# Loads from GpSimd with one packet per transfer and engine

## The chip, the cores and the metric

The kernel runs on one core of a Trainium2 chip. The metric is the device time of one execution, in microseconds (us). The core has five engines that matter here, each with its own list of instructions: TensorE (PE; its weight loads are listed apart as PEld), VectorE (DVE), ScalarE (ACT), GpSimd (POOL) and SyncE (SP). Transfers between the chip's memory (DRAM) and the core's on-chip memory (SBUF) are carried out by 16 DMA engines. They are asked for by GpSimd, whose transfers may change the number type on the way, or by SyncE[...].

## The reference

Two layers follow each other. Batch is 8, heads 8, sequence length 576, head size 64, so the model width is 512.

```
# 1: attention with a running bias
scores = q @ k.T / 8
cum    = cumsum(max(s, 0))                      # over the sequence
scores = scores + min(-(cum[i] - cum[j]), 0)    # and -1e9 above the diagonal
x      = softmax(scores) @ v                    # heads side by side: (8, 576, 512)

# 2: mixing of the 64 lowest frequencies
X      = rfft(x over the sequence)[:, :64]      # real and imaginary parts Xr, Xi
Yr[m]  = Xr[m] @ w_r[m] - Xi[m] @ w_i[m]        # one 512 x 512 matrix pair per frequency m
Yi[m]  = Xr[m] @ w_i[m] + Xi[m] @ w_r[m]
u      = x + irfft(Y)
out    = u + max(u @ w_ch, 0)
```

All inputs and the output are float32. The two weights `moe_w_r` and `moe_w_i` have 64 x 512 x 512 numbers each, 64 MB each. Each is used once, so all 128 MB have to be read in one execution. q, k and v are 9 MB each.

## The kernel before

The attention runs over 32 pairs of heads: 4 groups `g` of two heads, and in each group 8 batches. `n` counts the pairs. For a pair the kernel transposes q and k on TensorE (`transposes`, L324), forms the scores in two halves (`scores`, L359 and L365; the last 64 rows apart in `scores4`, L340), takes exponentials on ScalarE (L373), multiplies by v (`av`, L394), and divides by the sums on VectorE (L399 to L404). `fft` (L418) turns the result into frequencies.

The mixing is cut by the 512 input features, in 4 groups of 128 that are the groups of the attention, and by the 64 frequencies, in 8 chunks `c`. `modes(g, c)` (L441) multiplies one group and chunk by four weight tiles: real or imaginary part, and even or odd frequencies. A group's products can start when the attention of its eight pairs is done, so they lie one group behind (`mode_steps`), among the pairs of the next group. The products of the last group, `g = 3`, come after the last pair, mixed with the products by `w_ch` (L602) that have no other place. Then follow the inverse transform (L693), the last products, the sum, and the stores (L748), issued by SyncE.

**The loads.** Every q, k, v and weight tile is loaded by GpSimd, through the function `load` (L213 to L217). These transfers turn float32 into bf16 or fp16 on the way. `loads_qkv(n)` makes four of them per pair: q and k as 128 partitions of 9 rows that lie together, 2304 bytes read and 1152 written per partition, and two for v, each with two pieces of 512 bytes read and 256 written per partition. `loads_tails(g)` loads the last 64 rows of v, in pieces of 256 bytes read and 128 written. `loads_w` loads weight tiles: 128 partitions times 4 frequencies, each a row of 512 numbers, 2048 bytes read and 1024 written. There are 128 weight tiles of 512 KB (counted as written). The weight of the last product, `wch_sb`, is loaded once by a line of its own (L552), also by GpSimd.

**The order.** At each pair `n` the loop issues the loads of pair `n + 3`, mixed evenly with as many weight tiles as `on_chip[n]` allows. Weight tiles go to two rings of 11 and 6 buffers (`WA`, `WB`) and, for the first eight, to places that are still unused. GpSimd issues in this fixed order. It waits where a buffer is still being read, and, by the framework's semaphores, each of its transfers waits until the eighth transfer before it has landed.

SyncE has a queue of its own. At the start it loads constants. During the pairs it copies two rows of the running sum into row 64 of `qtA` and row 0 of `qtB` (`cum_rows`, L311 and L312), 1.1 KB each. At the end it moves `y_sb` and `v_sb` into `yv` (`spread`, L466) and stores the output.

Of the kernel before, what the change touches and what calls it, by code (L numbers as in the profile page):

```python
# [18 lines left out]
def kernel(  # L19
# [11 lines left out]
    nc = tc.nc  # L31
# [181 lines left out]
    def load(*lists):  # L213

        todo = [((i + 0.5) / len(l), x) for l in lists for i, x in enumerate(l)]
        for _, (dst, src) in sorted(todo, key=lambda t: t[0]):
            nc.gpsimd.dma_start(out=dst, in_=src)  # L217

# [24 lines left out]
    nc.sync.dma_start(out=negm32, in_=d_negm)  # L245
    first, second, tails0 = loads_qkv(0), loads_qkv(1), loads_tails(0)
    load(first[:2])
    load(loads_w(W0), first[2:] + tails0 + second)
    nc.sync.dma_start(out=Ff_sb, in_=d_Ff.rearrange("(T p) c -> p T c", p=P))
    nc.sync.dma_start(out=ident16h, in_=d_ident16h)  # L250
# [20 lines left out]
    with tc.tile_pool(name="cum_psum", bufs=1, space=PSUM) as cpsum:  # L271
# [5 lines left out]
            out=cum, data0=spos, data1=zer, initial=0.0, op0=ALU.add, op1=ALU.add  # L277
# [16 lines left out]
        for x in range(2):  # L294
            rows = slice(NL * x, NL * x + NL)
            nc.vector.tensor_copy(
                out=cumt4[rows, :], in_=cumt_sb[rows, NK, x::2]
# [222 lines left out]
    with tc.tile_pool(name="sc_psum", bufs=2, space=PSUM) as scpool, \  # L520
# [3 lines left out]
        transposes(0, 0)  # L524
        transposes(0, 1)
        load(loads_qkv(2))
        pad_p()
        for n in range(N):
# [355 lines left out]
```

The softmax here doesn't subtract the row's maximum and nothing guards it: scores larger than these inputs give would overflow.

## Time and profile before

| | |
|---|---|
| time, median of 3 runs | 456.14 us (455.82 to 456.61) |
| span of the profiled execution | 453.8 us |
| busy: PE / PEld / DVE / ACT / POOL | 340.4 / 218.6 / 241.0 / 221.9 / 183.0 us |
| GpSimd's transfers, count | 265 |
| weight tile, GpSimd's time to issue it | about 0.75 us |
| weight tile, median from issue to landing | 11.9 us |
| q tile, median from issue to landing | 9.9 us |
| bias row `qtA`, median from issue to landing | 4.6 us |
| read from DRAM / written to DRAM | 164.56 MB / 9.44 MB |

How to read it. Busy time says how long an engine had work in hand, not whether the work was on the path that sets the end. The row of slices cuts the span in 40 equal parts of 11.3 us; the DMA digit is the mean busy share of the 16 DMA engines in tenths, and below it stand the GB/s moved, counted by the bytes as written. In the table of queues, q0 holds GpSimd's transfers, q1 SyncE's, q8 and q14 the fetching of the program. What the profile calls packets there are its records of single pieces of data: one for each row that a transfer moves, and one for each write to a semaphore. Time to landing includes the time that a transfer stands in the queue behind others.

### The profile page before, as it was taken

The numbers are of one execution on the slowest core, as the hardware profiler recorded it, in microseconds if no ns is written. First come the engines' busy times: TensorE is split into PE (matmuls) and PEld (weight loads), VectorE is DVE, ScalarE is ACT, GpSimd is POOL, SyncE is SP. The second block draws the span as 40 slices with busy tenths as digits, with TensorE's granted clock in tenths as the row PEclk, the third lists the DMA queues.
The fourth block names the chain that finished last, engine by engine and source line by source line (L and its number), as shares of the span: only waits on it lengthen the run. The fifth ranks groups of instructions, "written<-read, shape, count | busy, mean of one in ns | idle before, by whom it ended". The sixth has DMA issues, their size and how long they took to land.

```text
span 453.8 us, 10370 instructions
## 1 busy us (share of the span) xinstructions
PE 340.4 (75%) x4233; PEld 218.6 (48%) x4265; DVE 241.0 (53%) x535; ACT 221.9 (49%) x390; POOL 183.0 (40%) x269
## 2 busy tenths in 40 slices
PE   1779887976563979836677857688889678879995
PEld 1456665654342656624445535456554335534332
DVE  7775665753242656723436434446655443562796
ACT  1585877464242656724435444455551323431774
POOL 6655554554344565434364444444433231200000
PEclk9996999998576889968878899889996986999999
DMA  9999999999999999999999999999999999995688
GB/s 176 200 203 203 202 201 204 202 204 204 205 204 202 201 203 202 205 205 204 202 196 203 204 204 203 204 203 202 206 207 208 207 206 206 207 214 109 232 298 317
DMA packets 108511, 93.75 MB, mean 207 GB/s; under 512 B 28384, under 2 KB 103648, under 8 KB 108464
## 3 DMA queue, kind: packets, MB, share of 16 engines
q0 software_dynamic: 98960, 81.81, 113.8%
q1 hardware_dynamic: 9504, 11.29, 7.8%
q8 instruction: 33, 0.54, 0.4%
q14 instruction: 14, 0.11, 0.1%
HBM read 164.56 MB, written 9.44 MB: 383 GB/s over the span
## 4 chain that ended last, share of the span: by engine, by line
DMA 51%; PE 31%; DVE 8%; issue 4%; POOL 2%; ACT 2%; SPq 0%; DVEq 0%; POOLq 0%; ACTq 0%
DMA w_sb<-in_moe_w_i_dram 21%; DMA q<-in_q_dram 15%; DMA w_sb<-in_moe_w_r_dram 11%; PE sc_ps L365 4%; PE av_ps L394 4%; PE z_ps L602 3%; PE yp L441 3%; PE sc_ps L359 3%; PE tr_ps L324 3%; DMA k<-in_k_dram 2%; PE z_ps L693 2%; PE g_ps L652 2%; PE ft_ps L418 2%; PE u_ps L712 2%; PE u_ps L693 1%
## 5 line engine op out<-in xcount | busy, mean ns | idle before, releaser
L373 ACT ACTIVATE p_sb<-sc_ps,cumt_sb 128x576 f16<-128x576 f32 (+1 forms) x256 | 141.7, 635 | 45.6 <-PE sc_ps L365 45.0
L217 POOL DMA_DIRECT2D w_sb<-in_moe_w_i_dram x60 | 45.1, 751 | 85.0 <-PE yp L441 37.6
L217 POOL DMA_DIRECT2D w_sb<-in_moe_w_r_dram x60 | 45.3, 757 | 63.5 <-DMA w_sb<-in_moe_w_r_dram 28.2
L217 POOL DMA_DIRECT2D v<-in_v_dram x72 | 50.8, 708 | 32.0 <-DMA w_sb<-in_moe_w_r_dram 7.4
L324 PE MATMUL tr_ps<-ident,q 64*64 64x64 bf16 x576 | 17.5, 210 | 54.3 <-DMA q<-in_q_dram 54.3
L359 PE MATMUL sc_ps<-negm,ident 128*128 128x256 bf16 x256 | 55.5, 303 | 0.2
L327 DVE COPY qtA<-tr_ps 64x576 bf16<-64x576 bf16 x32 | 23.8, 743 | 49.6 <-PE tr_ps L324 49.5
L441 PE MATMUL yp<-w_sb,xs 128*32 128x512 bf16 x480 | 36.5, 406 | 14.1 <-DMA w_sb<-in_moe_w_i_dram 11.1
L344 ACT ACTIVATE p<-sc_ps,cumt 128x64 f16<-128x64 f32 x32 | 10.0, 313 | 74.3 <-PE sc_ps L340 74.3
L394 PE MATMUL av_ps<-v,p_sb 128*128 128x65 f16 x1024 | 44.5, 198 | 0.0
L394 PEld LDWEIGHTS <-p_sb 128*128 128x128 f16 x1024 | 39.5, 100 | 4.9 <-issue 0.8
L327 DVE COPY ktA<-tr_ps 64x576 bf16<-64x576 bf16 x32 | 24.0, 749 | 33.6 <-PE tr_ps L324 33.6
L324 PEld LDWEIGHTS <-q 64*64 64x64 bf16 x576 | 13.7, 123 | 57.0 <-DMA q<-in_q_dram 56.3
L365 PE MATMUL sc_ps<-qtB,ktB 128*128 128x64 bf16 (+2 forms) x160 | 34.9, 324 | 3.5 <-issue 2.4
L365 PE MATMUL sc_ps<-qtA,ktA 65*128 65x512 bf16 (+2 forms) x192 | 36.5, 299 | 0.7 <-DMA qtA<-ncum_sb 0.7
L399 DVE TENSOR_REDUCE den<-av_ps 128x5 f32<-128x10 f32 x64 | 10.8, 169 | 49.1 <-PE av_ps L394 48.9
L441 PEld LDWEIGHTS <-xs 128*32 128x32 bf16 x512 | 22.6, 170 | 23.8 <-issue 19.8
L404 DVE TENSOR_TENSOR x_all<-av_ps,rcp 128x320 f16<-128x320 f32 x64 | 31.5, 491 | 2.2
L327 ACT COPY ktB<-tr_ps 64x576 bf16<-64x576 bf16 x32 | 20.3, 634 | 20.3 <-DVE ktA L327 19.4
L365 PEld LDWEIGHTS <-ktB 128*128 128x128 bf16 x192 | 22.4, 117 | 14.8 <-issue 6.3
L324 PE MATMUL tr_ps<-ident,k 64*64 64x64 bf16 x576 | 17.3, 209 | 15.3 <-DVE qtB L327 10.7
L602 PE MATMUL z_ps<-wch_sb,xs 128*128 128x512 f16 x96 | 26.1, 421 | 0.2 <-DVE xs L596 0.2
(117 smaller groups left out, 534.8 us busy)
## 6 DMA issues: line engine op xcount, KB each, us to landing
w_sb<-in_moe_w_r_dram POOLq DMA_DIRECT2D x60, 512.0 KB, 11.9
w_sb<-in_moe_w_i_dram POOLq DMA_DIRECT2D x60, 512.0 KB, 11.9
q<-in_q_dram POOLq DMA_DIRECT2D x32, 144.0 KB, 9.9
k<-in_k_dram POOLq DMA_DIRECT2D x32, 144.0 KB, 10.0
v<-in_v_dram POOLq DMA_DIRECT2D x72, 64.0 KB, 9.7
out_dram<-r_sb SPq DMA_DIRECT2D x16, 256.0 KB, 2.2
out_dram<-r_w SPq DMA_DIRECT2D x16, 256.0 KB, 2.6
x_all<-in_moe_w_i_dram POOLq DMA_DIRECT2D x3, 512.0 KB, 9.9
```

The source lines that it names most:

```text
L217: nc.gpsimd.dma_start(out=dst, in_=src)
L324: nc.tensor.transpose(ps[rows, r, :], src[rows, r, :], ident16[rows, rows])
L327: copy(out=dst[n % NQ][rows, :].rearrange("d (p r) -> d p r", r=R), in_=ps[rows].rearrange("d r p -> d p r"),)
L359: nc.tensor.matmul(ps[:, bass.ds(w * S, W)], ident16, negm[:, bass.ts(r, W)], start=True, stop=False, skip_group_check=True,)
L365: nc.tensor.matmul(ps[:, c0 : c0 + i1 - i0], keys[:, w, r, :], qt[:, i0:i1], start=False, stop=True, skip_group_check=True,)
L373: nc.scalar.activation(out=pt[:, poff[x] : poff[x] + S - w * W], in_=ps[:, w * S : (w + 1) * S - w * W], func=ACTF.Exp, bias=cumt_sb[:, x, ...
L394: nc.tensor.matmul(ps[:, I, r : r + NCH], lhsT, rhs, start=(i == 0), stop=(i == len(todo) - 1), skip_group_check=True,)
L399: nc.vector.tensor_reduce(out=den, in_=ps[:, :, 0 : VW : NCH], axis=mybir.AxisListType.X, op=ALU.add)
L404: nc.vector.tensor_tensor(out=x_all[:, g, b, :, D * h : D * h + D], in0=ps[:, :, 1 : NCH], in1=rcp.unsqueeze(2).to_broadcast([P, NT, D]), ...
L441: nc.tensor.matmul(ps[32 * cg : 32 * cg + 32, :], cols[:, c0 : c0 + 32, c * MC + 2 * cg + par], wt[(g, c, ri, par)][:, cg, :], start=(x == ...
L602: nc.tensor.matmul(z[:, x, :], xts[i][:, x, dt, :], wch_sb[:, dt, :], start=(dt == 0), stop=(last and dt == DT - 1), skip_group_check=True,)
L693: nc.tensor.matmul(dst[x][r, :], G_sb[rows, bass.ds(T * P, r.stop - r.start)], yv[rows, bb, which, :], start=start, stop=True, skip_group_ ...
```

## The change

In `load`, each transfer gets one more argument:

```
-            nc.gpsimd.dma_start(out=dst, in_=src)
+            nc.gpsimd.dma_start(out=dst, in_=src, single_packet=True)
```

A transfer is split over the DMA engines, and on each engine into descriptors, one for each piece of memory that is contiguous on both sides. [...] a weight tile has 128 x 4 / 16 = 32 data pieces per engine, a q or k tile 8, a v tile 16, a tail tile 32. It is for having fewer packets to begin and to end. The instructions of all engines, their order and their waits stay the same, 266 on GpSimd before and after. The load of `wch_sb` (L552) and SyncE's transfers are not touched.

## The prediction

> **What bounds the kernel now.** I first read the slices of the span and the queues, because a change to transfers can matter only where the 16 DMA engines are the limit.
>
> ```profile
> DMA  9999999999999999999999999999999999995688
> GB/s 176 200 203 203 202 201 204 202 204 204 205 204 202 201 203 202 205 205 204 202 196 203 204 204 203 204 203 202 206 207 208 207 206 206 207 214 109 232 298 317
> DMA packets 108511, 93.75 MB, mean 207 GB/s; under 512 B 28384, under 2 KB 103648, under 8 KB 108464
> ...
> q0 software_dynamic: 98960, 81.81, 113.8%
> q1 hardware_dynamic: 9504, 11.29, 7.8%
> ...
> DMA 51%; PE 31%; DVE 8%; issue 4%; POOL 2%; ACT 2%; SPq 0%; DVEq 0%; POOLq 0%; ACTq 0%
> ```
>
> The DMA engines are 90% or more busy in every slice until slice 36, about 408 us, and nearly all of it is q0, GpSimd's queue. The rate is flat at 200 to 208 GB/s whatever the compute does. These bytes are counted on the bf16 side; the sources are f32, so twice as much is read, about 410 GB/s. A flat rate under changing work is a limit of the transfers themselves.
>
> Who waits for them, over the pairs from 66 to 330 us:
>
> ```profile
> PE tr_ps L324 <- DMA q<-in_q_dram: 54.3, 15, 8.1
> PE yp L441 <- DMA w_sb<-in_moe_w_i_dram: 4.9, 5, 2.4
> PE tr_ps L324 <- DMA k<-in_k_dram: 4.6, 4, 1.2
> ```
>
> TensorE stands 64 us in that stretch for q, k and weights. They come late because they queue behind the weights on the same ring. Now the pure weight stretch, GpSimd's issues in order of time, and the transfers between 340 and 390 us:
>
> ```profile
> 347.87 0.74 POOL L217 DMA_DIRECT2D w_sb<-in_moe_w_r_dram  x1 [1.84 <-DMA w_sb<-in_moe_w_r_dram]
> 350.47 0.74 POOL L217 DMA_DIRECT2D w_sb<-in_moe_w_i_dram  x1 [1.86 <-DMA w_sb<-in_moe_w_i_dram]
> 353.00 0.74 POOL L217 DMA_DIRECT2D w_sb<-in_moe_w_i_dram  x1 [1.78 <-PE yp L441]
> 355.50 0.74 POOL L217 DMA_DIRECT2D w_sb<-in_moe_w_r_dram  x1 [1.76 <-PE yt_ps L625]
> ```
>
> ```profile
> DMA packets 10366, 10.33 MB, mean 207 GB/s; under 512 B 330, under 2 KB 10347, under 8 KB 10363
> ...
> w_sb<-in_moe_w_i_dram POOLq DMA_DIRECT2D x9, 512.0 KB, 19.8
> w_sb<-in_moe_w_r_dram POOLq DMA_DIRECT2D x8, 512.0 KB, 19.8
> ```
>
> One weight tile goes out every 2.53 us (7.63 us for three) and lands 19.8 us later: 19.8 / 2.53 = 7.8 are in flight. The program lets each transfer of GpSimd wait for the eighth before it, so GpSimd paces itself by the landings, and the queue never runs dry. The issue itself (0.74 us) is hidden: GpSimd idles 1.8 us before each.
>
> Last, where this ends. In TensorE's timeline:
>
> ```profile
> 372.85 0.57 PE L441 MATMUL yp<-w_sb,xs 128*32 128x512 bf16 x4 [2.04 <-DMA w_sb<-in_moe_w_i_dram]
> ...
> 390.79 1.12 PE L441 MATMUL yp<-w_sb,xs 128*32 128x512 bf16 x16
> ...
> 411.04 0.69 PE L441 MATMUL yp<-w_sb,xs 128*32 128x512 bf16 x8
> ```
>
> 372.85 us is the last time that TensorE waits for a weight. The later mode products start without such a wait; 372.85 to the end, 81 us, is TensorE, VectorE and ScalarE work and the stores. So the kernel is a DMA stream of 373 us and a compute part of 81 us.
>
> [...]
>
> [...] A weight tile is 128 partitions x 4 rows, 32 rows of 2048 B read per engine. At 27.2 GB/s these take 32 x 75.3 ns = 2.41 us; the cadence is 2.53 us. The 0.12 us over are 3.75 ns per row[...]. The trace's packet records show one more thing: each is one row, median 98 ns for a weight row, 41 ns for a v row (512 B read), 22 ns for a 4-byte semaphore write. If one such write of 22 ns stands in the 0.12 us, 3.1 ns per row are left. [...]
>
> **The change part by part.** *Removed:* packet ends between the rows of one transfer. q0 has 98960 records; 265 transfers x 16 semaphore writes are 4240 of them, so 94,720 are rows, 5920 per engine. Per engine a weight tile gives 32 rows, a q or k tile 8, a v tile 16, a tail tile 32[...]. `wch` (L552) keeps the default. What counts is what is moved before 372.85 us: 104 of the 128 weight tiles (three groups of 32 and chunks 0 and 1 of the last group) 3328 rows, 64 q and k tiles 512, 64 v tiles 1024, 8 tails 256, 5120 rows per engine. One gap per transfer stays (240 transfers), so 4880 gaps go. At 3.75 ns that is 18.3 us, at 3.1 ns 15.1 us. I take 16.5 us.
>
> *What of it reaches the end.* The stream has no idle slice before 373 us and TensorE waits 64 us for it, so the stream's saving shortens the stretch one for one; TensorE keeps about 48 us of waiting. In the last chunks its DMA waits are 5.9 us, where the stream saves under 2 us (13 tiles from 340 to 373 us at 0.11 us). After 372.85 us nothing is saved. 456.1 - 16.5 = 439.6; I forecast 440.
>
> *Added:* coarser turns. A packet of one weight tile holds an engine for 32 x 75.3 ns = 2.4 us instead of 79 ns. SyncE's bias rows (L311, L312) are the ones with readers: 32 + 32, landing in 4.6 us now. With one packet to wait for before the data and one before the semaphore they land in up to 4.6 + 2 x 2.4 = 9.4 us. Each is issued when the scores of the pair before last have been read, and is needed a pair later: 11 us and more in the stretch bound by the stream; some 8 us in the early pairs, 6.3 us apart, where up to 1 us a pair could show. But the queue is full by then too, and the compute has caught up with it only at 67 us, so I put it at nothing, at most 5 us. Program fetches (q8, 33 of 16 KB) wait the same 2.4 us[...]; nothing.
>
> *GpSimd's issue:* the same 265 instructions in the same order; 0.74 us each, beside 1.8 us idle. Nothing, even if it grew by half.
>
> *Unknown:* whether a long packet keeps the pipeline full at its end. The records overlap now: 98 ns long, 79 ns apart, so about 19 ns of the next row run under the last. If packets of a transfer don't overlap, each of the 240 costs a gap. From below this is 0 to 22 ns (5 us in all), from above the whole quiet landing of a transfer, 2.2 us for the stores at the end, which would be absurd beside eight in flight. The break-even is 16.5 us / 240 = 69 ns: less than one weight row.
>
> **The rivals.**
> - *Part only.* Some of the 3.1 to 3.75 ns belongs to each descriptor[...], and half of it stays: 456.1 - 8 = 448. [...]
> - *No change.* The overhead is wholly per descriptor, or the memory is the limit: 456. For it: a flat rate fits a memory limit too. [...]
> - *Slower.* A gap at each packet's end that is longer than 69 ns[...]. At 125 ns a transfer: 240 x 0.125 = 30 us, less 16.5, 470 us. [...] Against it: eight transfers are queued[...].
>
> **How the numbers follow.** Most of the overhead gone, 435 to 444: 0.46. Part only, 444 to 455: 0.15. No change: 0.12. Slower: 0.27, half of it below 467 us. The low end takes all of the 18.3 us and 1 to 2 us more, 435. The high end, 467, leaves out the worse half of the slow case. Faster 0.61, same 0.12, slower 0.27.
>
> **What would show it.** In the profile after: weight issues 2.42 us apart instead of 2.53 between 340 and 370 us; 214 to 216 GB/s in place of 206 to 208; TensorE's wait for q down by some 12 us; the last wait for a weight near 356 us; the 81 us behind it unchanged. An unchanged 2.53 us speaks for the second rival. A longer cadence, or weight records that no longer overlap, speaks for the third; so would bias rows that TensorE waits for. I am wrong if the gap between packets costs more than a row[...].

## The result, and the profile after

The changed kernel takes 455.81 us (median of 4 runs, 455.45 to 456.52) beside 455.98 us before (455.54 to 456.61): a ratio of 0.9995, 95% interval 0.9981 to 1.0009. Forecast were 440 us and a range of 435 to 467. The time lies in the range, but a clear gain was forecast and there is none. What came is the second rival, "no change".

The slices and GpSimd's queue in the profile of the changed kernel:

```profile
DMA  9999999999999999999999999999999999995688
GB/s 178 201 203 203 202 202 203 202 204 204 205 204 202 200 203 202 205 205 204 202 197 204 204 204 204 204 203 202 206 207 208 206 207 206 206 214 104 232 298 316
DMA packets 108511, 93.75 MB, mean 207 GB/s; under 512 B 28384, under 2 KB 103648, under 8 KB 108464
...
q0 software_dynamic: 98960, 81.81, 113.8%
```

The number of records on q0 is the same to the unit, 98960, and so are the classes by size: in both traces 66048 of 1024 B (weights, `wch_sb` among them), 8192 of 1152 B (q and k), 16384 of 256 B and 4096 of 128 B (v), one for each piece that is contiguous on both sides, and 4240 semaphore writes. So is the share of 113.8%. GpSimd has 269 instructions in both profiles. TensorE's waits between 66 and 330 us:

```profile
PE tr_ps L324 <- DMA q<-in_q_dram: 53.5, 14, 7.8
PE yp L441 <- DMA w_sb<-in_moe_w_i_dram: 5.1, 3, 2.5
...
PE tr_ps L324 <- DMA k<-in_k_dram: 3.5, 3, 1.3
```

62 us against 64 before; the forecast wanted 12 us less. GpSimd's issues in the pure weight stretch:

```profile
347.75 0.74 POOL L217 DMA_DIRECT2D w_sb<-in_moe_w_r_dram  x1 [1.78 <-DMA w_sb<-in_moe_w_r_dram]
350.41 0.74 POOL L217 DMA_DIRECT2D w_sb<-in_moe_w_i_dram  x1 [1.92 <-PE z_ps L602]
352.93 0.74 POOL L217 DMA_DIRECT2D w_sb<-in_moe_w_i_dram  x1 [1.78 <-PE yp L441]
355.42 0.74 POOL L217 DMA_DIRECT2D w_sb<-in_moe_w_r_dram  x1 [1.75 <-PE yt_ps L625]
```

Three tiles in 7.67 us, 2.56 us each; before it was 2.54 (7.63 for three). The release named behind each differs, for instance TensorE's `z_ps` at 350.41, but the distance doesn't: by the program's semaphores each waits for the landing of the eighth transfer before, and TensorE's event probably just fell near it. A weight row is still recorded with a median of 98 ns, a v row with 41, a semaphore write with 22. SyncE's bias rows, which the prediction expected a long packet to delay, land in 4.6 us as before.

So nothing that was read here about a transfer has moved. The prediction took it that the argument makes one packet of all the rows that an engine gets from one transfer, and that the time lost per row is lost at a packet's end. Both were the author's assumptions; no trace had shown them. Three explanations were open. *A:* the argument doesn't act on transfers that change the number type. *B:* the rows were joined, but the lost time belongs to each row and not to the packet. *C:* the argument changes nothing on the chip for any of these loads. And one premise needed a test of its own: that there is time lost per row at all, and not a fixed limit of the memory's rate.

### The profile page after: what moved, and what is told of

Read it like the earlier page. It is cut to its first block, busy times and chain, and to the rows that moved or that the text cites. A ratio compares the mean times of both kernels' runs of the same rounds, so it can differ in the third digit from the quotient of the medians.

```text
span 453.7 us, 10402 instructions
## 1 busy us (share of the span) xinstructions
PE 344.1 (76%) x4265; PEld 219.0 (48%) x4265; DVE 240.4 (53%) x535; ACT 222.2 (49%) x390; POOL 182.9 (40%) x269
## 3 DMA queue, kind: packets, MB, share of 16 engines
q0 software_dynamic: 98960, 81.81, 113.8%
## 4 chain that ended last, share of the span: by engine, by line
DMA 51%; PE 29%; DVE 8%; issue 7%; POOL 3%; ACT 2%; SPq 0%; DVEq 0%; POOLq 0%; ACTq 0%
DMA w_sb<-in_moe_w_i_dram 19%; DMA w_sb<-in_moe_w_r_dram 14%; DMA q<-in_q_dram 13%; PE sc_ps L365 4%; PE av_ps L394 3%; PE sc_ps L359 3%; PE tr_ps L324 2%; POOL w_sb L217 2%; DMA k<-in_k_dram 2%; PE z_ps L602 2%; PE yp L441 2%; PE z_ps L693 2%; PE g_ps L652 2%; PE u_ps L712 2%; PE u_ps L693 1%
## 5 line engine op out<-in xcount | busy, mean ns | idle before, releaser
L217 POOL DMA_DIRECT2D w_sb<-in_moe_w_r_dram x60 | 45.4, 757 | 62.7 <-DMA w_sb<-in_moe_w_r_dram 27.1
L359 PE MATMUL sc_ps<-negm,ident 128*128 128x256 bf16 x256 | 56.9, 309 | 0.2
L365 PE MATMUL sc_ps<-qtB,ktB 128*128 128x512 bf16 (+2 forms) x192 | 45.7, 357 | 0.0
L217 POOL DMA_DIRECT2D k<-in_k_dram x32 | 17.6, 551 | 20.4 <-DMA w_sb<-in_moe_w_r_dram 7.4
```

Of the source, the lines that this page charges most:

```text
L217: nc.gpsimd.dma_start(out=dst, in_=src, single_packet=True)
L359: nc.tensor.matmul(ps[:, bass.ds(w * S, W)], ident16, negm[:, bass.ts(r, W)], start=True, stop=False, skip_group_check=True,)
L365: nc.tensor.matmul(ps[:, c0 : c0 + i1 - i0], keys[:, w, r, :], qt[:, i0:i1], start=False, stop=True, skip_group_check=True,)
```

## Experiments

**Is the time lost per row?** Two kernels change only where a weight tile is read from, so that the same bytes come in other rows. Both put the weights in the wrong places.

```
# "..." stands for what is left out
# long_rows: 512 features of one frequency, 8 KB together per partition
-   ... src[c * MC + par : (c + 1) * MC : 2, g * P : (g + 1) * P, :].rearrange("m p e -> p m e") ...
+   ... src[16 * g + 2 * c + par].rearrange("(p r) e -> p r e", r=4) ...

# half_rows: first halves of 1024 feature rows, 8 rows of 1 KB per partition
-   ... (the same line)
+   m = min(16 * g + 2 * c + par, NM - 2)
+   two = src[m : m + 2].rearrange("m d e -> (m d) e").rearrange("(p r) e -> p r e", r=8)
+   ... two[:, :, :256] ...
```

> The kernel before with each weight tile taken from 512 features of one frequency, 8 KB that lie together per partition, in place of 4 rows of 2 KB: the same bytes and instructions, 8 pieces per engine in place of 32, the weights in the wrong places. If the 3.1 to 3.75 ns are paid per row: 24 rows x 104 tiles x 3.1 to 3.75 ns = 7.7 to 9.4 us faster, about 447.5 us, weights 2.45 us apart. If the memory is the limit: 456 us, 2.53 us apart.

> The kernel before with each weight tile taken in 8 rows of 1 KB (the first halves of 1024 feature rows of two frequencies) in place of 4 of 2 KB: the same bytes and instructions, 64 pieces per engine in place of 32, the weights in the wrong places. Paid per row: 32 x 104 x 3.1 to 3.75 ns = 10.3 to 12.5 us slower, 466 to 469 us, weights 2.63 to 2.65 us apart. A memory limit: no change, unless half rows are harder on the memory.

Measured: long rows 446.49 us, ratio 0.9791 (0.9775 to 0.9807), 9.4 us less. Half rows 471.65 us, ratio 1.0353 (1.0336 to 1.0371), 15.7 us more. First TensorE's products with the weights in long rows, around the last wait for a weight (363.80), then GpSimd's issues in that stretch; then the same of half rows, where the wait for the same tile is at 386.51 and two more come later:

```profile
360.59 1.25 PE L438 MATMUL yp<-w_sb,xs 128*32 128x512 bf16 x12
363.80 0.46 PE L438 MATMUL yp<-w_sb,xs 128*32 128x512 bf16 x4 [1.97 <-DMA w_sb<-in_moe_w_i_dram]
381.79 1.12 PE L438 MATMUL yp<-w_sb,xs 128*32 128x512 bf16 x16
```

```profile
342.19 0.53 POOL L214 DMA_DIRECT2D w_sb<-in_moe_w_i_dram  x1 [1.72 <-PE yp L438]
344.63 0.53 POOL L214 DMA_DIRECT2D w_sb<-in_moe_w_i_dram  x1 [1.91 <-PE yp L438]
347.08 0.53 POOL L214 DMA_DIRECT2D w_sb<-in_moe_w_r_dram  x1 [1.92 <-PE z_ps L599]
349.54 0.53 POOL L214 DMA_DIRECT2D w_sb<-in_moe_w_r_dram  x1 [1.93 <-PE z_ps L599]
```

```profile
386.51 0.65 PE L440 MATMUL yp<-w_sb,xs 128*32 128x512 bf16 x4 [2.18 <-DMA w_sb<-in_moe_w_i_dram]
404.45 1.12 PE L440 MATMUL yp<-w_sb,xs 128*32 128x512 bf16 x16
...
427.89 0.46 PE L440 MATMUL yp<-w_sb,xs 128*32 128x512 bf16 x4 [1.11 <-DMA w_sb<-in_moe_w_i_dram]
430.73 0.45 PE L440 MATMUL yp<-w_sb,xs 128*32 128x512 bf16 x4 [0.53 <-DMA w_sb<-in_moe_w_i_dram]
```

```profile
363.10 0.88 POOL L216 DMA_DIRECT2D w_sb<-in_moe_w_i_dram  x1 [1.83 <-DMA w_sb<-in_moe_w_i_dram]
365.75 0.88 POOL L216 DMA_DIRECT2D w_sb<-in_moe_w_i_dram  x1 [1.77 <-PE yp L440]
368.35 0.88 POOL L216 DMA_DIRECT2D w_sb<-in_moe_w_r_dram  x1 [1.72 <-PE yt_ps L624]
371.00 0.87 POOL L216 DMA_DIRECT2D w_sb<-in_moe_w_r_dram  x1 [1.77 <-PE z_ps L601]
```

Weights are 2.45 us apart in long rows and 2.63 in half rows, against 2.54 (over 12 to 14 tiles of that stretch 2.46, 2.66 and 2.55). The wait that was the last one before moves from 372.85 to 363.80 and to 386.51 us, by -9.1 and +13.7. What follows it is 81.0 us of the span of 444.8 with long rows, as before, and 82.6 of 469.1 with half rows: the last two tiles come late there too, and TensorE waits another 1.11 and 0.53 us for them. The stream is the limit, its rows cost time, and the cost reaches the end. A limit that only counts bytes is out. Whether the time of a row is lost in the memory or in the DMA engine, these two kernels don't tell.

**Does the argument join rows?** The next kernels do nothing but load: no attention and no mixing, and zeros are stored. Eight stages of 20 transfers follow each other, eight in flight, and SyncE copies a row of 1.1 KB over and over as a probe. Each of these kernels ran once; what is compared are stages of one execution.

```
STAGES = [("a", "bf16", 512, 4, False), ("b", "bf16", 512, 4, True),    # type, elements of a row,
          ("c", "f32",  512, 4, False), ("d", "f32",  512, 4, True),    # rows per partition,
          ("e", "bf16", 128, 6, False), ("f", "bf16", 128, 6, True),    # one packet
          ("g", "f32",  128, 6, False), ("h", "f32",  128, 6, True)]
...
nc.gpsimd.dma_start(out=dst, in_=src, single_packet=one)                # from f32
nc.sync.dma_start(out=got, in_=row)                                     # after every second
```

> Only loads, no attention and no mixing (the output is zeros): eight stages of 20 GpSimd loads each, back to back, 8 in flight, with a 1.1 KB SyncE copy after every second one. Stages in pairs, default and one packet: bf16 from f32 in 2 KB rows, f32 to f32 in 2 KB rows, bf16 from f32 in 512 B rows, f32 to f32 in 512 B rows. Theory A (the argument has no effect on transfers that change the type): the f32 pairs differ, by 0.1 us of 2.5 a transfer with 2 KB rows and by over 10% with 512 B rows, and SyncE's copies land later beside one-packet loads; the bf16 pairs don't. Theory B (the packets are joined, but the overhead is per row and not per packet): no pair differs in rate, but SyncE's copies land 1 to 5 us later beside the one-packet stages. Theory C (the argument changes nothing for any of GpSimd's direct loads): no pair differs in rate or in the landing of SyncE's copies.

One stretch inside each of stages a to h, with its length, the busy times of VectorE and GpSimd, the clock, the share of the DMA engines and the GB/s written:

```profile
12.00:32.00 20.00, 0.00 (x0) 5.87 (x8) 1.00 1.25 206
64.00:84.00 20.00, 0.00 (x0) 5.93 (x8) 1.00 1.25 206
120.00:140.00 20.00, 0.00 (x0) 5.24 (x7) 1.00 1.03 386
175.00:195.00 20.00, 0.00 (x0) 5.24 (x7) 1.00 1.03 386
227.00:239.00 12.00, 1.23 (x8) 9.02 (x12) 1.00 1.83 180
247.00:257.00 10.00, 0.61 (x4) 7.31 (x10) 1.00 1.83 180
275.00:289.00 14.00, 1.23 (x8) 7.95 (x11) 1.00 1.03 291
299.00:309.00 10.00, 0.46 (x3) 4.12 (x5) 1.00 1.03 290
```

The pairs are equal: 206 and 206, 386 and 386, 180 and 180, 291 and 290. A wanted the f32 pairs to differ, and they don't; but equal rates would also fit rows that are joined and pay one by one. The probe lands with a median of 4.5 us in both of stages a and b, 5.0 in both c and d, 6.3 and 6.1 in g and h (three and two copies). B wanted it later beside one packet. The records themselves say more. Queue q0 in the four stretches of c, d, g and h, each as count of records, MB and share of the DMA engines:

```profile
q0 software_dynamic: 2003, 7.72, 102.5%
```

```profile
q0 software_dynamic: 1995, 7.71, 102.3%
```

```profile
q0 software_dynamic: 1159, 4.06, 102.5%
```

```profile
q0 software_dynamic: 824, 2.90, 102.6%
```

7.72 MB in at most 2003 records are at least 3850 bytes each, where a row has 2048; 4.06 MB in 1159 are 3500, where a row has 512. In the trace every data record of these stages is of 4096 bytes, the rest are semaphore writes. So for loads that keep the type a record isn't a row, as it is in the kernel studied, but several rows joined: two of 2 KB, eight of 512 B. The default joins there already, the trace can show joined rows, and the argument does not make the records longer, so A is out. For the loads that change the type a record is one row with and without it: 4148 records and 4.12 MB in each of a and b.

B could still hold for those if their rows were joined and only recorded one by one. The start times of the probe's own records settle it. On each of the 16 engines a copy of SyncE is one piece of 72 bytes and then one semaphore write. The delay from the one to the other is compared with the time of GpSimd's records. Averaged over the engines, the delay has a median over the copies of 83 and 84 ns in a and b, where a row takes 80 ns; 165 and 166 in c and d, where a record of 4096 B takes 170; 27 and 27 in e and f (three copies each), where a row takes 23. In the next kernel it is 193 and 194 beside records of 4608 B that take 189, and 93 and 93 beside rows that take 89. (Beside f32 rows of 512 B and less the copies are too few and scatter.) So the delay is about the time of one record of GpSimd's, also where the record holds two rows (165 beside 170 ns): the engine came back to SyncE's queue after one record, and "packet" means here what was moved between two such turns. A packet of 32 rows in stage b would by an estimate from these delays have made it about 2.5 us (32 x 80 ns). In the kernel studied the bias rows show the same between 70 and 330 us, a mean of 76 ns before and 76 after (48 copies each). No rows were joined there, and B is out.

**More sizes, and one packet on long rows.** The stages are those before with other rows; the kernel is `long_rows` with the argument added in `load`.

```
STAGES = [("a", "f32", 576, 3, False), ("b", "f32", 576, 3, True), ("c", "f32", 256, 4, False), ("d", "f32", 256, 4, True),
          ("e", "f32", 64, 6, False), ("f", "f32", 64, 6, True), ("g", "bf16", 576, 3, False), ("h", "bf16", 576, 3, True)]
```

> Only loads, output zeros: eight stages of 20 loads in pairs, default and one packet: f32 to f32 in rows of 2304 B, of 1 KB, of 256 B, and bf16 from f32 in rows of 2304 B. The first stages run showed f32 loads recorded in pieces of 4096 B that hold 2 rows of 2 KB or 8 rows of 512 B, so a record is a packet and the default already joins rows there. Theory C (the argument has no effect on the chip): in each pair the size of the records, the GB/s and the landing of SyncE's copies are the same; 1 KB and 256 B rows are recorded in 4096 B pieces in both. If it does act where a default packet is smaller than the transfer: records of over 4096 B in the one-packet stages, and other landings. If joining saved the overhead: 2304 B rows, alone in their packets, would have a larger overhead per row than the 9.4 to 9.6 ns that 2 KB and 512 B rows have; if the overhead is the row's, again 9 to 10 ns.

```profile
8.00:28.00 20.00, 0.00 (x0) 6.82 (x10) 1.00 1.02 390
55.00:75.00 20.00, 0.00 (x0) 6.69 (x9) 1.00 1.03 391
99.00:110.00 11.00, 0.00 (x0) 5.24 (x7) 1.00 1.03 348
130.00:150.00 20.00, 0.31 (x2) 9.90 (x13) 1.00 1.03 347
161.00:172.00 11.00, 0.46 (x3) 8.76 (x11) 1.00 1.03 218
178.00:186.00 8.00, 0.00 (x0) 8.00 (x10) 1.00 1.04 218
196.00:216.00 20.00, 0.00 (x0) 6.87 (x9) 1.00 1.22 207
238.00:258.00 20.00, 0.00 (x0) 7.62 (x10) 1.00 1.22 207
```

The stretches lie in stages a to h in order. Again all pairs are equal, to 1 GB/s. The records are of 4608 bytes (two rows of 2304) in a and b and of 4096 in c to f, and one row each in g and h, with and without the argument. (The expectation took the rows of 2304 B to be alone in their packets; they come in twos. In e and f GpSimd's issue, busy 8.76 of 11 and 8.00 of 8 us, is close to the limit as well.)

> The kernel with weights in rows of 8 KB that lie together (wrong places), and one packet per transfer and engine on all loads through the same function. Theory C (no effect): 446.5 us as without the argument, weights 2.45 us apart, SyncE's bias rows landing in 4.6 us. If the argument joins these 8 rows and the overhead were the packet's: 104 tiles x 7 x 3.8 ns = 2.8 us less, and in 64 KB packets the bias rows land later.

445.67 us, ratio 0.9776 (0.9755 to 0.9797) to the kernel before; long rows alone had 0.9791 (0.9775 to 0.9807). The intervals overlap, ten tiles take 24.53 us (341.70 to 366.23) against 24.55 without the argument (342.19 to 366.74), and the bias rows land in 4.9 us against 4.8. A gain of 2.8 us, ratio 0.973, is outside the interval. C holds here too.

**What a row costs.** The stage kernel once more, with default loads only, in five row lengths with a change of type and three without.

```
STAGES = [("a", "bf16", 2048, 1, False), ("b", "bf16", 1024, 2, False), ("c", "bf16", 512, 4, False),
          ("d", "bf16", 256, 4, False), ("e", "bf16", 128, 8, False),
          ("f", "f32", 2048, 1, False), ("g", "f32", 512, 4, False), ("h", "f32", 128, 8, False)]
```

> Only loads, output zeros: eight stages of 20 default loads. bf16 from f32 in rows of 8 KB, 4 KB, 2 KB, 1 KB and 512 B read, then f32 to f32 in rows of 8 KB, 2 KB and 512 B. An overhead per row of 3.1 to 3.75 ns over 27.2 GB/s per engine: a 512 KB tile takes 2.44 to 2.46 us in 8 KB rows against 2.53 in 2 KB rows; 1 KB rows take 41 ns each, 512 B rows 22 to 23 ns each. A memory limit: the time per byte is the same in 8, 4 and 2 KB rows, 2.53 us a tile.

```profile
12.00:32.00 20.00, 0.00 (x0) 4.47 (x9) 1.00 1.07 213
64.00:84.00 20.00, 0.00 (x0) 5.71 (x9) 1.00 1.13 211
115.00:135.00 20.00, 0.00 (x0) 5.93 (x8) 1.00 1.25 206
165.00:180.00 15.00, 1.08 (x7) 8.97 (x11) 1.00 1.46 196
193.00:205.00 12.00, 0.61 (x4) 6.11 (x9) 1.00 1.83 181
225.00:245.00 20.00, 0.15 (x1) 4.46 (x8) 1.00 1.01 420
275.00:295.00 20.00, 0.00 (x0) 5.37 (x8) 1.00 1.03 386
327.00:340.00 13.00, 0.00 (x0) 6.19 (x7) 1.00 1.03 290
```

Time per row and engine is the row's written bytes x 16 / GB/s. From it go, for loads that change the type, the transfer's semaphore record of 22 ns spread over its rows (0.3 to 2.8 ns), and the bytes read at 27.2 GB/s. That is the rate of the prediction's working, and the stages give it too: with the semaphore taken off, rows of 8 KB and of 512 B differ by 7680 bytes and 282.6 ns, which is 27.2 GB/s (f32 to f32, with nothing taken off: 283.9 ns, 27.1 GB/s). The rates of 2304 and 1024 B without a change of type are from the kernel before this one. As the GB/s are whole numbers, what is left is uncertain by up to 0.7 ns in the longest rows and 0.1 in the shortest.

| bytes read per row | changing the type: GB/s, left per row | f32 to f32: GB/s, left per row | rows per record, f32 to f32 |
|---|---|---|---|
| 8192 | 213: 307.7 - 301.2 - 2.8 = 3.7 ns | 420: 312.1 - 301.2 = 10.9 ns | 1 |
| 4096 | 211: 155.3 - 150.6 - 1.4 = 3.3 ns | | |
| 2304 | | 391: 94.3 - 84.7 = 9.6 ns | 2 |
| 2048 | 206: 79.5 - 75.3 - 0.7 = 3.5 ns | 386: 84.9 - 75.3 = 9.6 ns | 2 |
| 1024 | 196: 41.8 - 37.6 - 0.7 = 3.5 ns | 348: 47.1 - 37.6 = 9.5 ns | 4 |
| 512 | 181: 22.6 - 18.8 - 0.3 = 3.5 ns | 290: 28.2 - 18.8 = 9.4 ns | 8 |

A row costs 3.3 to 3.7 ns where the type changes, and about 9.5 ns where it doesn't, whatever its length. (The 10.9 of the longest row holds a semaphore record, which is 9 ns in these stages and 1.1 ns on each of eight rows.) In the f32 column records hold one to eight rows and the cost per row stays, so it is not the record, or packet, that pays. If a packet's end cost the time, eight rows of 512 B would share one cost, and that stage would run near the rate of the 8 KB stage instead of 290 against 420 GB/s. The rows of 2 KB and 512 B are read in the same pattern in both types, so where one type pays 3.5 ns and the other 9.5, reading the memory can't be the whole of it.

## Why the prediction was wrong, point by point

- *What bounds the kernel:* right, and now shown. The same bytes in longer or shorter rows moved the wait for one and the same tile by -9.1 and +13.7 us and the span by -9.0 and +15.3.
- *The size of the loss per row:* about right, with a slip. 7.63 us for three tiles is 2.54 us and not 2.53, and the same working then gives 4.2 ns per row, or 3.5 with the semaphore write taken off, in place of 3.75 and 3.1. Five row lengths give 3.3 to 3.7. The 27.2 GB/s per engine in that working had no measurement beside it when it was written; `stages_rows` gives it (7680 bytes in 282.6 ns).
- *How many rows lie before 372.85 us:* 8 tiles too few. After that wait 64 `yp` matmuls are left, four to a tile, so 16 of the 128 tiles: 112 had come, the last group's chunks 0 to 3, and not 104. The forecast's gaps become 5128 and its saving 15.9 to 19.2 us. That is not why it failed.
- *"The stream's saving shortens the stretch one for one":* right. With 112 tiles long rows should have saved 8.3 to 10.1 us, and saved 9.1 at the wait and 9.4 in all; that is 3.4 ns per row. Half rows should have cost 11.1 to 13.4 and cost 13.7 at the wait, 3.8 ns per row. In all they cost 15.7, over the range of 10.3 to 12.5 that was expected of them: the 8 tiles and the two late waits (1.6 us) make up most of that.
- *"One gap per transfer stays, so 4880 gaps go":* this is the step that failed. No gap went. The records are the same single rows, an engine still turns to SyncE's queue after each of them (76 ns), and the term of 16.5 us measured 0.2 us, with an interval from -0.4 to 0.9.
- *The reason under it, that the time is lost at a packet's end:* an assumption of the author's, taken along because there was a loss for each row. The stages show otherwise: in f32 loads, where records do hold several rows, each row pays, 9.4 ns in records of eight and 9.6 in records of two. A loss measured per row couldn't tell one from the other in a kernel in which each record was one row.
- *Added costs* (bias rows later, program fetches, a gap at a packet's end): none came, since no packet became longer. They are untested, not refuted; so is the rival "slower". The later bias rows rested on a packet keeping the engine from SyncE's queue; the probe's delays beside longer records fit that (165 ns beside f32 records of 4096 B, 83 beside rows of 80 ns).
- *The rival "no change"* had the right time and half of the reason: the loss is per row, but not a limit of the memory's rate. It got 0.12, because the 3.75 ns per row were taken for a loss per packet, which was an estimate and not shown.

Shown is that the argument changes neither records, rates nor the probe in eight pairs of stages, nor records, rates and bias rows in two kernels. Not shown is where it is lost on the way, or whether converted rows that were truly joined would be cheaper; no run here made such a packet.

## What to carry to other kernels

Before a setting is priced, ask of the profile whether its cause can be told from its neighbours: a loss per row is not yet a loss per packet. Where the DMA engines are busy all through, as here, a transfer's time was its bytes plus 3.3 to 3.7 ns for each row that changed the type, so what helped was longer rows: 8 KB in place of 2 KB was worth 9.4 us of 456 here. A layout that gives long rows and the right result would have to put neighbouring features on one partition, that is in different products, and wasn't built.

## What the runs showed of the hardware

Loads that keep f32 pay more per row than loads that turn f32 into bf16, about 9.5 ns against 3.5, so that in 2 KB rows the stages read more per second while converting (2 x 206 = 412 GB/s) than while not (386). And SyncE's small copy lands in 4.5 us beside converting loads in 2 KB rows, in 6.1 to 6.3 us beside f32 loads in 512 B rows, both times with eight transfers of GpSimd's in flight; at the end of the last stage, as that queue ran dry, it took 1.6 us (`stages_flag`, median of the eight copies between 300 and 322 us). A DMA engine with work from both queues went from one to the other after each record: the small copy's semaphore write followed its data by about the time of one record of GpSimd's, from 27 ns beside 512 B rows that are converted to 166 ns beside f32 records of 4096 B.
